# First matmul of the last two token tiles partly in seven block products, a reordered head, and padded value rows, in a fused attention and MLP kernel

## The chip, the cores and the metric

The kernel runs on one core of one Trainium2 chip. Times are device microseconds (us) of that core; with one core it is also the slowest core. Every run quoted here was fast, with a mean granted TensorE clock of 0.988 to 1.0. A "profile" is one execution recorded by the hardware profiler; its span is 1.8 us shorter than the time of the same execution.

Engines are called as the profile calls them: PE is TensorE, DVE VectorE, ACT ScalarE, SP the engine whose queue issues the transfers.

## The reference, cut to what matters

```python
# q, k, v: (8 batches, 8 heads, 576 tokens, 64), float32
q_s = softmax(q, axis=-1); k_s = softmax(k, axis=2)
kv  = einsum('bhsd,bhse->bhde', k_s, v)
x   = einsum('bhsd,bhde->bhse', q_s, kv)          # -> (8, 576, 512)
xn  = (x - mean(x)) / sqrt(var(x) + 1e-6) * g_ln  # over the 512 columns
out = x + relu(xn @ w_ch1) @ w_ch2                # 512 -> 2048 -> 512
```

## The kernel before

Each batch is a tile of 512 tokens. The 64 tokens that each of the eight batches has left over form a ninth tile, "batch 8", done last. The mean is not subtracted from x but from the rows of w1 ("centring", on PE with a matrix of ones and on DVE with a subtraction), and the factor 1/sqrt(var) is applied at the end. Inputs of batch b+1 are loaded and its attention is done inside the matmuls of batch b.

The second matmul already uses the seven-product form (Strassen in Winograd's arrangement): operands cut into 2 x 2 blocks, seven block products in place of eight, and sums of blocks on DVE. The first matmul is plain:

```python
def mm1(c, split, open_=()):
    ...
    for n, m in enumerate(order):                  # 16 output tiles of 128 x 512
        def f(...):
            for ko in range(k0, KO1):              # KO1 = 4
                nc.tensor.matmul(bank[gi], w1_sb[:, ko, m * P : m * P + P], xt[:, ko], ...)
        ids.append(plan.add("PE", 0.216 * (KO1 - k0), f, r=..., w=[(bk, gi)]))
        relu_evac(m, bank[gi], (bk, gi), eng(n))   # PSUM -> hT, mostly on ACT
        if split and n in (HK, KO2 - 1):
            sums(0 if n == HK else 4)              # block sums of hT for the second matmul
```

All work is written as tasks with an engine, a planned time, reads and writes. A list scheduler turns them into one fixed order; each engine then executes its own part of it strictly in that order. A priority (`cls`), a planned delay (`slack`), a planned transfer size (`mb`) or an `after=` changes only that order, and it can change it far from where it was written.

```python
class Plan:
    def add(self, eng, dur, fn, r=(), w=(), cls=1, land=0.0, mb=0.0, after=(), slack=0.0): ...
    def emit(self):
        seq = self.order()                         # the list scheduler
        for i in seq: ... self.tasks[i][2]()       # issue

def load(dst, src, w, mb):                         # one queue, on SP, in order
    gate[1] = plan.add("SP", 0.55, lambda: nc.sync.dma_start(dst, src), w=w, mb=mb, land=0.65,
                       after=tuple(gate[0]) + ((gate[1],) if gate[1] is not None else ()))
```

The part of the input side that the argument needs, for a batch in the steady state. `gate[0]` holds the loads of a batch behind the transposing transfer of the batch before it:

```python
if steady:
    gate[0] = state["eqT"]                         # the eqT transpose of the batch before
lq = [load_half(b, q, hf) for hf in range(2)]      # SP: load q
for hf in range(2):
    queries(hf, lq[hf])                            # ACT: exp; DVE: sum, reciprocal, eq = eq * rzq
...
state["eqT"] = (dma_t(),)                          # SP: eqT <- eq, a transposing transfer
# later: PE k-v product, ACT/DVE kve scaling, PE eqT x kve, ACT copies to xsT,
# SP: x <- xsT, a transposing transfer; DVE: bn_stats of x
```

The parts of the head that the change reorders are `load_w1` (a w1 tile scaled on ACT or DVE) and `centre_w1`:

```python
def load_w1(blk):
    on_act = ((1,), (0, 1, 3), (1,), (1, 3))[blk]  # which of four tiles ACT scales
    ...
def centre_w1(blk):
    def f():
        for ko in range(KO1):
            nc.tensor.matmul(bank, ones, w1_sb[:, ko, cs], start=(ko == 0), stop=(ko == KO1 - 1))
    plan.add("PE", 0.216 * KO1, f, ...)
    state["nm"] = plan.add("ACT", ..., lambda: nc.scalar.copy(nm, bank), ...)
    ...                                            # DVE: w1 = w1 - nm
```

The softmax here doesn't subtract the row's maximum and nothing guards it: scores larger than these inputs give would overflow.

Of the kernel before, what the change touches and what calls it, by code (L numbers as in the profile page):

```python
# [13 lines left out]
FP16 = mybir.dt.float16  # L14
BF16 = mybir.dt.bfloat16
U32 = mybir.dt.uint32
AF = mybir.ActivationFunctionType
# [122 lines left out]
def kernel(  # L140
# [29 lines left out]
    def sb(shape, dt, name):  # L170
        return persist.tile(shape, dt, name=name, tag=name)
# [10 lines left out]
    ek = [sb([P, 2, JT, P], BF16, f"ek{i}") for i in range(2)]  # L182
    vb = [sb([P, 2, JT, 2, VW], FP16, f"vb{i}") for i in range(2)]
    eq = [sb([P, 2, JT, P], BF16, f"eq{i}") for i in range(2)]
# [70 lines left out]
    def load_w1(blk):  # L255
        on_act = ((1,), (0, 1, 3), (1,), (1, 3))[blk]
        cls = 0.5 if blk else 0
        for kp in range(2):
            s = nxt("stg", NST)
            load(stg[s][:, :1024].rearrange("p (a n) -> p a n", a=2),  # L260
                 w1_src[:, 2 * kp : 2 * kp + 2, blk * 512 : blk * 512 + 512], sk(s), 0.524 if blk or kp else 0.72)
            for a in range(2):
                ko = 2 * kp + a
                after = state["kve"] if blk == 1 and (kp or ko not in on_act) else ()
                if blk == 2:
                    after = (state["nm"],) if ko in on_act else state["ev"][1]
                dst = w1_sb[:, ko, blk * 512 : blk * 512 + 512]
                src = stg[s][:, a * 512 : a * 512 + 512]
                gk = g_sb[:, ko : ko + 1]
                if ko in on_act:  # L270
                    plan.add("ACT", act_t(512, 0.1), lambda dst=dst, src=src, gk=gk: nc.scalar.activation(  # L271
                        dst, src, AF.Copy, scale=gk), r=sk(s) + [("g", ko)], w=[("w1", blk, ko)], after=after, cls=cls)
                else:
                    plan.add("DVE", dve_t(512, 2), lambda dst=dst, src=src, gk=gk: nc.vector.tensor_scalar_mul(
                        dst, in0=src, scalar1=gk), r=sk(s) + [("g", ko)], w=[("w1", blk, ko)], after=after, cls=cls)

    def centre_w1(blk):

        if blk:
            gi = nxt("pa", 4)  # L280
            bank, bk = pa[gi], ("pa", gi)
        else:
            bank, bk = pg[opened[2]], ("pg", opened[2])
        cs = slice(blk * 512, blk * 512 + 512)
        wk = [("w1", blk, ko) for ko in range(KO1)]
        def f():
            for ko in range(KO1):
                nc.tensor.matmul(bank, ones, w1_sb[:, ko, cs], start=(ko == 0), stop=(ko == KO1 - 1))  # L288
        plan.add("PE", 0.216 * KO1, f, r=wk + ["ones"], w=[bk], cls=0)
        state["nm"] = plan.add("ACT", act_t(512), lambda: nc.scalar.copy(nm, bank), r=[bk], w=["nm"], cls=-0.5)  # L290
        def sub(k0, k1, m0, m1):
            n = (m1 - m0) * P
            c0 = blk * 512 + m0 * P
            return plan.add("DVE", dve_t((k1 - k0) * n, 2), lambda: nc.vector.tensor_tensor(  # L294
                w1_sb[:, k0:k1, c0 : c0 + n], w1_sb[:, k0:k1, c0 : c0 + n],
                nm[:, m0 * P : m0 * P + n].unsqueeze(1).to_broadcast([P, k1 - k0, n]), op=ALU.subtract),
                r=["nm"] + wk, w=[("w1c", 4 * blk + m, k) for m in range(m0, m1) for k in range(k0 // 2, k1 // 2)], cls=0)

        if blk == 0:
            state["sub"] = sub(0, 2, 0, 4)  # L300
            return lambda: sub(2, 4, 0, 4)
        sub(0, 4, 0, 1)
        sub(0, 4, 1, 4)

# [18 lines left out]
    def attn(b, kind, between=None, exps=(), sums_=(), kvs=()):  # L323
# [44 lines left out]

        def keys(hf, s):
            plan.add("ACT", act_t(QW), lambda: nc.scalar.activation(  # L370
                ek[u][:, hf].rearrange("p j (s d) -> p s j d", s=2), sv(s), AF.Exp),
                r=sk(s), w=[("ek", u, hf)], cls=cls, slack=late, after=exps)
# [10 lines left out]
        def kv(hs):  # L383
            ab = [[nxt("pa", 4) for _ in range(2)] for _ in hs]
            def f():
                for n, hf in enumerate(hs):
                    for j in range(JT):
                        for e in range(2):
                            for i in range(2):
                                r0, c0 = R * e, D * i  # L390
                                nc.tensor.matmul(pa[ab[n][e]][c0 : c0 + D, :VW], ek[u][r0 : r0 + R, hf, j, c0 : c0 + D],  # L391
                                                 vb[u][r0 : r0 + R, hf, j, i, :], start=(j == 0), stop=(j == JT - 1))
            ids = []
            kcls = 0 if not steady else 0.35 if b > 2 else -0.6
            plan.add("PE", 0.1 + 0.42 * len(hs), f, r=[("ek", u, h) for h in hs] + [("vb", u, h, i) for h in hs for i in range(2)],
                     w=[("pa", a) for x in ab for a in x], cls=0, slack=SLACK if steady else 0.2, after=kvs)
            for n, h in enumerate(hs):
# [58 lines left out]
        if kind == "first":  # L456
            lq, lk, lv = [load_half(b, t, 0, x) for t, x in ((q, 0), (k, 0), (v, 0))]
            queries(0, lq)
            keys(0, lk)
            values(0, lv)  # L460
            lq = load_half(b, q, 1)
            load_w1(0)
            pe_t_evac(0, *pe_t(0))
            kves = kv([0])
            xT([0])
            queries(1, lq, kves[:1])
            t1 = pe_t(1)
            between()
            pe_t_evac(1, *t1, (state["sub"],))
            lk, lv = [load_half(b, t, 1) for t in (k, v)]  # L470
            keys(1, lk)
            values(1, lv)
            cnt["pa"] = 0
            state["kve"] = kv([1])
            state["sub2"]()
            xT([1])
            return xT_last
# [58 lines left out]
    def relu_evac(m, bank, bk, eng):  # L536
# [4 lines left out]
        if eng == "ACT":  # L541
            plan.add("ACT", act_t(512), fa, r=[bk], w=[("hT", m)], cls=0)
        else:
            plan.add("DVE", dve_t(512), fd, r=[bk], w=[("hT", m)], cls=0)

# [35 lines left out]

    def sums(k0):
        n = 4
# [3 lines left out]
        h12, h22 = hT[:, kh, 0:256], hT[:, kh, 256:512]  # L587
        lo, hi = [("hT", k0 + i) for i in range(n)], [("hT", HK + k0 + i) for i in range(n)]
        sk = lambda i: [("S", i, k0 + j) for j in range(n)]
        def tt(i, a, b, op, r):  # L590
            plan.add("DVE", dve_t(256 * n, 2), lambda: nc.vector.tensor_tensor(S[i][:, ks], a, b, op=op), r=r, w=sk(i), cls=0.3 if k0 else 0.45)  # L591
        tt(0, h21, h22, ALU.add, lo + hi)
# [34 lines left out]
    def mm2_split(c):  # L627
# [3 lines left out]
        if c == B:  # L631
            ga[1] = (pa[0][:, 0:256], ("pa", 0))
        o1, o2 = nxt("ot", NOT), nxt("ot", NOT)
        rk = lambda t0: [(stk, "r", 2 * t0), (stk, "r", 2 * t0 + 1)]
        hk = lambda k0: [("hT", k0 + k) for k in range(HK)]
        skey = lambda i: [("S", i, k) for k in range(HK)]
        wk = lambda k0: [("w2", k0 + k) for k in range(HK)]
        tkey = lambda i: [("T", i, k) for k in range(HK)]
        h = lambda k, t0, i: hT[:, k, 256 * t0 + i * P : 256 * t0 + i * P + P]
        A = {"11": (lambda k, i: h(k, 0, i), hk(0)), "12": (lambda k, i: h(HK + k, 0, i), hk(HK)),  # L640
             "22": (lambda k, i: h(HK + k, 1, i), hk(HK))}
        for i in range(4):
# [5 lines left out]

        def product(a, b, g, first, last):
            (fa, ka), (fb, kb) = A[a], Bm[b]  # L650
            for i, ks in [(0, range(0, 4)), (0, range(4, HK)), (1, range(HK))]:
                def f(i=i, ks=ks):
                    for k in ks:
                        nc.tensor.matmul(g[i][0], fa(k, i), fb(k),  # L654
                                         start=(first and k == 0 and (i == 0 or g[0][1] != g[1][1])), stop=(last and k == HK - 1),
                                         skip_group_check=True)
                plan.add("PE", 0.1093 * len(ks), f, r=[ka[k] for k in ks] + [kb[k] for k in ks], w=[g[i][1]])

# [27 lines left out]
        add_x(2, gb, 1, 256)  # L686
        product("S3", "T3", ga, False, False)
        state["stats"] = (final(o2, 1, ga, 2, 1),)
        if c == B:
            plan.add("SP", 0.62, lambda: nc.sync.dma_start(last_rows(1)[:, :, 256:512], ot[o2][:, :, 256:512]),  # L690
                     r=[("ot", o2, 1)], mb=0.26, land=2.0, cls=0)
        product("S4", "22", gb, False, True)
        final(o1, 1, gb, 1, 0)
# [14 lines left out]
    def mm2(c):  # L708
# [4 lines left out]
        for k0 in range(0, KO2, 4):  # L713
            for j in range(J):
                def f(k0=k0, j=j):
                    for kk in range(k0, k0 + 4):
                        nc.tensor.matmul(pg[gis[j]], hT[:, kk, j * P : j * P + P], w2_sb[:, kk, :],  # L717
                                         start=(kk == 0), stop=(kk == KO2 - 1))
                i = plan.add("PE", 0.864, f, r=[("hT", kk) for kk in range(k0, k0 + 4)] + [("w2", kk) for kk in range(k0, k0 + 4)], w=[("pg", gis[j])])
                if j == 0:  # L720
# [22 lines left out]
    def warm(n):  # L743
        return plan.add("PE", 0.43 * n, lambda: zeros(pg[3], True)(n), r=["zero"], w=[("pg", 3)], cls=0)


# [28 lines left out]
    for b in range(B):  # L775
        if b:
            state["tok"] = tokens(b, 0.7 if b > 1 else 0.35, stats=state["stats"])
        if b == B - 1:
            tokens(8, 0.7, stats=state["stats"])
        rstd = state.get("rstd")  # L780
        ids = mm1(b, b > 0, () if b else opened)
        if b == 0:
# [11 lines left out]
        before = (ids[-1], rstd)  # L794
    mm1(8, True)
    mm2_split(8)
# [36 lines left out]
```

## Time and profile before

| | before |
|---|---|
| time, median of 3 runs | 279.06 us (278.26 to 279.40) |
| the profiled execution | 277.7 us, span 275.9 |
| PE, DVE, ACT busy | 97%, 72%, 61% of the span |
| start of batch 1 on PE | 52.25 us |
| k-v product of batch 7 starts on PE | 201.52 us |
| end of PE's work | 272.08 us |

The stretches of the profiled execution, by one view of all engines (start and end in us, length, then for PE, PEld, DVE, ACT, POOL the busy us and the instructions, the granted clock, the busy share of the DMA engines, GB/s):

```profile
46.00:72.00 26.00, 26.00 (x268) 14.45 (x266) 23.76 (x47) 19.20 (x35) 0.00 (x0) 1.00 0.93 255
72.00:118.00 46.00, 46.00 (x456) 29.09 (x446) 36.14 (x76) 33.72 (x55) 0.00 (x0) 1.00 0.83 220
118.00:202.00 84.00, 83.96 (x828) 54.03 (x818) 62.70 (x133) 56.43 (x91) 0.00 (x0) 1.00 0.78 205
```

Read the first busy number against the length: from 46 to 202 us PE has work for all but 0.04 us.

### The profile page before, as it was taken

Reading aid. Unit: us, or ns where it says so; the run is one execution under the profiler, and the core shown is the slowest. Engines: PE = TensorE matmul, PEld = TensorE weight load, DVE = VectorE, ACT = ScalarE, POOL = GpSimd, SP = SyncE. Lnnn points to the kernel's source line nnn. Section 1 sums busy time; section 2 is a strip of 40 time slices with the busy share of each in tenths; the row PEclk is TensorE's granted clock in tenths of the full one; section 3 lists DMA queues with packets and bytes.
Section 4 is the critical chain, followed back from the end, with each engine's and each line's share of the span. In section 5 each row is a group of like instructions: output and inputs, shape, how many; then the busy total and the mean of one; then the engine's idle time right before and its main releaser. Section 6 shows DMA issues by size and latency. Waiting matters only on the chain.

```text
span 275.9 us, 5670 instructions
## 1 busy us (share of the span) xinstructions
PE 268.4 (97%) x2324; PEld 163.7 (59%) x2324; DVE 198.5 (72%) x412; ACT 168.2 (61%) x274; POOL 1.7 (1%) x12
## 2 busy tenths in 40 slices
PE   8988999999999999999999999999999999999994
PEld 3433445446864587458745874578457845874583
DVE  1788998998769767966697669766976764742562
ACT  4678966788598693659466856685664076016500
POOL 2000000000000000000000000000000000000000
PEclk9999999999999999999999999999999999999999
DMA  7999999799989994499659965796544450022004
GB/s 257 361 386 387 388 388 233 184 330 256 319 265 187 280 334 48 143 216 389 75 153 185 395 100 154 160 394 124 154 86 77 78 154 0 0 64 90 1 4 152
DMA packets 55874, 54.83 MB, mean 199 GB/s; under 512 B 34596, under 2 KB 35112, under 8 KB 55848
## 3 DMA queue, kind: packets, MB, share of 16 engines
q1 hardware_dynamic: 55696, 54.34, 69.6%
q8 instruction: 18, 0.29, 0.4%
q10 hardware_dynamic: 152, 0.13, 0.1%
q14 instruction: 8, 0.07, 0.1%
HBM read 36.70 MB, written 9.44 MB: 167 GB/s over the span
## 4 chain that ended last, share of the span: by engine, by line
PE 91%; DMA 4%; SPq 1%; ACT 1%; DVE 1%; issue 0%
PE pg L575 43%; PE pg L654 35%; PE pg L717 5%; DMA stg<-in_v_dram 4%; PE pa L391 2%; PE pa L422 2%; PE pa L654 1%; PE pa L575 1%; SPq L238 1%; PE pa L288 1%; PE pg L553 1%; ACT hT L538 1%; PE pa L445 0%; PE pa L519 0%; DVE vb L377 0%; ACT w_sb L271 0%
## 5 line engine op out<-in xcount | busy, mean ns | idle before, releaser
L538 ACT ACTIVATE hT<-pg 128x512 f16<-128x512 f32 x134 | 78.8, 598 | 65.2 <-PE pg L575 64.8
L575 PE MATMUL pg<-xsT,w_sb 128*128 128x512 f16 x488 | 108.4, 379 | 0.8 <-ACT hT L538 0.8
L575 PEld LDWEIGHTS <-w_sb 128*128 128x128 f16 x568 | 54.8, 98 | 65.9 <-DVE w_sb L294 1.6
L654 PEld LDWEIGHTS <-S 128*128 128x128 f16 x512 | 49.6, 98 | 6.3 <-issue 0.4
L654 PE MATMUL pg<-T,S 128*128 128x256 f16 x368 | 41.9, 273 | 0.0
L654 PEld LDWEIGHTS <-hT 128*128 128x128 f16 x384 | 37.2, 98 | 7.8 <-issue 2.2
L591 DVE TENSOR_TENSOR S<-hT 128x1024 f16<-128x1024 f16 x32 | 21.8, 681 | 26.5 <-ACT hT L538 26.5
L664 DVE SCALAR_TENSOR_TENSOR cp<-pg,st,x 128x256 f32<-128x256 f32 x46 | 20.2, 479 | 14.2 <-PE pg L654 13.7
L664 DVE SCALAR_TENSOR_TENSOR ot<-pg,st,cp 128x256 f32<-128x256 f32 x47 | 20.5, 477 | 12.2 <-PE pg L654 12.0
L654 PE MATMUL pg<-w_sb,hT 128*128 128x256 f16 x248 | 29.2, 273 | 0.0
L527 DVE BATCH_NORM_STATS2 bst<-x 128x6 f32<-128x512 f16 x36 | 23.9, 666 | 4.8 <-DMA x<-xsT 4.8
L342 DVE TENSOR_REDUCE zq<-eq 128x18 f32<-128x1152 bf16 x16 | 21.5, 1344 | 4.7 <-ACT eq L340 4.7
L340 ACT ACTIVATE eq<-stg 128x1152 bf16<-128x1152 f32 x16 | 18.7, 1170 | 7.3 <-DMA stg<-in_q_dram 7.2
L346 DVE TENSOR_TENSOR eq<-eq,rzq 128x1152 bf16<-128x1152 bf16 x16 | 21.6, 1352 | 0.3
L370 ACT ACTIVATE ek<-stg 128x1152 bf16<-128x1152 f32 x16 | 18.7, 1170 | 3.0 <-DMA stg<-in_k_dram 3.0
L380 ACT CAST vb<-stg 128x1152 f16<-128x1152 f32 x15 | 17.6, 1174 | 4.4 <-DMA stg<-in_v_dram 4.3
L435 ACT CAST xsT<-pa 128x512 f16<-128x512 f32 x31 | 16.0, 592 | 3.0 <-PE pa L422 3.0
L654 PE MATMUL pg<-w_sb,S 128*128 128x256 f16 x128 | 15.3, 273 | 0.0
L717 PE MATMUL pg<-w_sb,hT 128*128 128x512 f16 x64 | 14.8, 380 | 0.0
L654 PE MATMUL pg<-T,hT 128*128 128x256 f16 x120 | 14.4, 273 | 0.0
L575 PE MATMUL pg<-xT,w_sb 128*128 128x512 f16 x64 | 14.0, 379 | 0.0
L740 PE MATMUL pg<-zero 128*128 128x512 f16 x33 | 10.6, 481 | 1.2 <-DVE zero L223 1.2
(71 smaller groups left out, 162.6 us busy)
## 6 DMA issues: line engine op xcount, KB each, us to landing
stg<-in_q_dram SPq DMA_DIRECT2D x16, 576.0 KB, 5.3
stg<-in_k_dram SPq DMA_DIRECT2D x16, 576.0 KB, 7.2
stg<-in_v_dram SPq DMA_DIRECT2D x16, 576.0 KB, 9.0
out_dram<-ot SPq DMA_DIRECT2D x33, 256.0 KB, 3.7
stg<-in_moe_w_ch_dram SPq DMA_DIRECT2D x16, 512.0 KB, 10.8
out_dram<-ot SPq DMA_DIRECT2D x1, 512.0 KB, 2.8
out_dram<-ot SPq DMA_DIRECT2D x1, 128.0 KB, 2.7
out_dram<-ot ACTq DMA_DIRECT2D x1, 128.0 KB, 2.2
```

The costliest lines, as they stand in the source:

```text
L340: plan.add("ACT", act_t(QW), lambda: nc.scalar.activation(e.rearrange("p j (s d) -> p s j d", s=2), sv(s), AF.Exp), r=sk(s), w=[("eq", u, ...
L342: plan.add("DVE", dve_t(QW), lambda: nc.vector.reduce_sum(zq[:, hf], eh, axis=AX.X), r=[("eq", u, hf)], w=[("zq", hf)], cls=qcls, after=sums_)
L346: plan.add("DVE", dve_t(QW), lambda: nc.vector.tensor_tensor(eh, eh, rzq[:, hf].to_broadcast([P, 2 * JT, D]), op=ALU.mult), r=[("rzq", hf) ...
L370: plan.add("ACT", act_t(QW), lambda: nc.scalar.activation(ek[u][:, hf].rearrange("p j (s d) -> p s j d", s=2), sv(s), AF.Exp), r=sk(s), w= ...
L380: plan.add("ACT", act_t(QW), lambda: nc.scalar.copy(vd, va), r=sk(s), w=[("vb", u, hf, i) for i in range(2)], cls=cls, slack=late, after=t ...
L527: plan.add("DVE", dve_t(512), lambda j=j: nc.vector.bn_stats(bst[:, j, :], x[:, j, :]), r=[(xk, j)], w=[("bst", j)], cls=cls, slack=2.0 if ...
L538: nc.scalar.activation(hT[:, m, :], bank, AF.Relu)
L575: nc.tensor.matmul(bank[gi], w1_sb[:, ko, m * P : m * P + P], xt[:, ko], start=(ko == 0), stop=(ko == KO1 - 1))
L591: plan.add("DVE", dve_t(256 * n, 2), lambda: nc.vector.tensor_tensor(S[i][:, ks], a, b, op=op), r=r, w=sk(i), cls=0.3 if k0 else 0.45)
L654: nc.tensor.matmul(g[i][0], fa(k, i), fb(k), start=(first and k == 0 and (i == 0 or g[0][1] != g[1][1])), stop=(last and k == HK - 1), ski ...
L664: nc.vector.scalar_tensor_tensor(dst[:, i, :], in0=g[i][0], scalar=sti[:, 4, 2 * t0 + i : 2 * t0 + i + 1], in1=src[:, i, :], op0=ALU.mult, ...
L717: nc.tensor.matmul(pg[gis[j]], hT[:, kk, j * P : j * P + P], w2_sb[:, kk, :], start=(kk == 0), stop=(kk == KO2 - 1))
```

## The change

It has three parts.

1. *Tail.* In batches 7 and 8, two of four groups of output tiles of the first matmul are computed as seven block products. Sums of w1 blocks (once) and of x blocks (per batch) are made on DVE, the intermediate sums leave PSUM through ACT copies and DVE additions. The readiness of hT, the first matmul's output, is now tracked by halves of its tokens, and one product and the statistics of batch 8 get another place in the order. The aim is less PE work.
2. *Head.* ACT takes more of the w1 scaling, several `after=` and planned times change, centring of the first block is cut in halves. The aim is that PE saturates earlier.
3. *Padding.* The rows of the value tile grow from 65 to 66 elements.

```diff
-    vb = [sb([P, 2, JT, 2, VW], FP16, f"vb{i}") for i in range(2)]
+    vb = [sb([P, 2, JT, 2, VW + 1], FP16, f"vb{i}") for i in range(2)]
...
-        on_act = ((1,), (0, 1, 3), (1,), (1, 3))[blk]
+        on_act = ((0, 1), (0, 1), (1,), (1, 3))[blk]
...
-                after = state["kve"] if blk == 1 and (kp or ko not in on_act) else ()
+                after = state["kve"] if blk == 1 and ko else ()
                 if blk == 2:
-                    after = (state["nm"],) if ko in on_act else state["ev"][1]
+                    after = (state["nm"],) if ko in on_act else (state["subs"],) if kp else state["ev"][1]
...
-        plan.add("PE", 0.216 * KO1, f, r=wk + ["ones"], w=[bk], cls=0)
+        for k0, k1 in ((0, 2), (2, 4)) if blk == 0 else ((0, 4),):
+            ...
+            plan.add("PE", 0.216 * (k1 - k0), f, r=wk[k0:k1] + ["ones"], w=[bk], cls=0)
...
-            queries(1, lq, kves[:1])
+            queries(1, lq, kves)
...
-            keys(1, lk)
+            keys(1, lk, (state["nm"],))
...
+    UNITS[7] = UNITS[8] = (0, 1)
+    def w1_sums(n, before): ...        # four sums of w1 blocks of group n, DVE, 128 x 512 each
+    def x_sums(c): ...                 # four differences of x blocks, DVE, 128 x 512 each
+    def mm1_seven(c):
+        ...
+            for u in us:
+                u.product("11", "11", 0, True, False)   # 4 matmuls of 256 columns into bank 0
+                u.copy(0, 0)                            # ACT: PSUM -> SBUF
+                u.product("12", "21", 1, True, True)
+                u.end(1, 0, 0, 0)                       # DVE: bank + copy -> hT, then the maximum with 0
+            for u in us:
+                u.product("S2", "T2", 0, False, False)
+                u.copy(0, 1)
+                u.product("S1", "T1", 2, True, False)
+                u.copy(2, 2)
+            for u in us:
+                u.product("S3", "T3", 0, False, False)
+                u.end(0, HK, 1, 2)
+                u.product("S4", "22", 2, False, True)
+                u.end(2, 0, 1, 1)
+            for u in us:
+                u.product("22", "T4", 0, False, True)
+                u.end(0, HK, 0)
...
-    mm1(8, True)
+    mm1_seven(8)
```

## The prediction

> **What bounds the kernel now.** I read the page first (shares, slices, chain of waits), then the chain in order of time, then the timelines of TensorE, VectorE (DVE) and ScalarE (ACT) in the head (0 to 36 us) and from 205 us to the end. The page says that TensorE (PE) is busy for 97% of the span and carries 91% of the chain:
>
> ```profile
> PE 268.4 (97%) x2324; PEld 163.7 (59%) x2324; DVE 198.5 (72%) x412; ACT 168.2 (61%) x274; POOL 1.7 (1%) x12
> PE 91%; DMA 4%; SPq 1%; ACT 1%; DVE 1%; issue 0%
> ```
>
> PE's busy time counts matmuls on a zero tile in the head, so I looked for where real work becomes continuous. PE's timeline (start us, us, what, count, idle before it):
>
> ```profile
> 13.89 1.03 PE L288 MATMUL pg<-w_sb,ones 128*128 128x512 f16 x4
> 15.86 0.68 PE L360 MATMUL pa<-ident_b,eq 128*128 128x128 bf16 x9 [0.94 <-DVE eq L346]
> 20.57 1.90 PE L575 MATMUL pg<-xsT,w_sb 128*128 128x512 f16 x8
> 23.23 1.90 PE L575 MATMUL pg<-xsT,w_sb 128*128 128x512 f16 x8 [0.76 <-ACT hT L538]
> 24.96 1.03 PE L288 MATMUL pa<-w_sb,ones 128*128 128x512 f16 x4
> 26.69 1.03 PE L288 MATMUL pa<-w_sb,ones 128*128 128x512 f16 x4
> ```
>
> The last gap ends at 23.23; from there to 272.09 the chain is PE almost without a break. So the time is (when PE saturates) + (PE work after it) + a short tail. In the tail the first matmul of the last two batches (L575) and the second (L654) alternate in the chain (start, length, what):
>
> ```profile
> 219.95 13.81 PE pg L575 x64
> 233.76 12.23 PE pg L654 x112
> 245.99 13.81 PE pg L575 x64
> ```
>
> Two prices follow: 13.81 / 64 = 0.2158 us per matmul with 512 columns, and 12.23 / 112 = 0.1092 us per one with 256. The second matmul is already in the seven-product form at this price. Halving the width costs 2 x 0.1092 - 0.2158 = 0.003 us per pair, almost nothing.
>
> In the head, PE waits for what DVE does in the wrong order. DVE's timeline:
>
> ```profile
> 11.51 0.48 DVE L274 TENSOR_SCALAR w_sb<-stg,g_sb 128x512 f16<-128x512 f32 x1 [0.61 <-DMA stg<-in_moe_w_ch_dram]
> 11.91 0.28 DVE L409 TENSOR_SCALAR kve<-pa,rz 128x64 f16<-128x64 f32 x1
> 15.83 0.75 DVE L377 CAST vb<-stg 128x576 f16<-128x576 f32 x1
> 22.35 0.49 DVE L274 TENSOR_SCALAR w_sb<-stg,g_sb 128x512 f16<-128x512 f32 x1 [0.87 <-DMA stg<-in_moe_w_ch_dram]
> 22.75 1.28 DVE L294 TENSOR_TENSOR w_sb<-w_sb,cp 128x512 f16<-128x512 f16 x2
> ```
>
> The subtraction at 22.75 is what PE's matmul at 23.23 needs, and it stood behind a weight scaling that waited 0.87 us for a transfer it has nothing to do with. (The waits view names ACT for that gap; ACT's relu of the bank ended earlier, so I take it for DVE.)
>
> **What the skill says.** "TensorE: Matmul & The Clock Gate", Back-to-back issue gap: warm, N/2.4 + 2.5 ns, so 109.2 ns at 256 and 215.8 at 512. The trace agrees to the digit (0.1092, 0.2158), not with the 131 ns which that section gives for sustained streams at 512. "VectorE: DVE Perf Modes", tier table: tensor_tensor on 16-bit SBUF data runs at 2x, with a PSUM operand at 1x. The trace agrees: the 128x1024 f16 sums at L591 take 0.69 us, the 128x512 operation out of PSUM at L731 0.68 (2.72 for four). "Advanced Engine Details and Errata", 2x-2p Requirements: source and destination need an outermost dimension even in both, or odd and equal in both. The v cast in the head reads one run of 576 and writes 9 rows of 64, so it doesn't qualify; at 0.75 us = 0.15 + 576/960 it indeed runs at 1x, while the L310 casts (1024 in one run on both sides) run at 2x, 0.69. Padding the row from 65 to 66 leaves 9 rows of 64.
>
> **The change, part by part.**
>
> *PE in the last two batches.* Of four groups of four output tiles, two use seven products of 4 matmuls of 256 columns: 7 x 4 x 0.1092 = 3.058 us, in place of 16 x 0.2158 = 3.453. Saved 0.395 a group, four groups in all: 1.58 us. This lies on the path, if nothing stalls PE.
>
> *ACT in one such batch.* Before: 16 relus of 0.60 in 13.81 us. After: 6 copies PSUM to SBUF, 4 relus out of place or in place on the DVE sums, 2 relus from PSUM, 8 direct relus: 20 x about 0.57 = 11.4 us, plus 0.5 of statistics in batch 7, against 13.03 us of PE. Full, but it fits.
>
> *DVE in one such batch.* Added: 6 sums out of PSUM x 0.68 = 4.1, two in-place maxima of about 0.3, four x differences of 0.42 (the L605 price): 6.4 us. Before, DVE was busy 15.4 us of 26.0 in batch 7 and less in batch 8, so it fits. The eight w1 sums (8 x 0.42 = 3.4 us) stand in the instruction order in batch 5's second half, where DVE idles 0.43, 1.16, 0.87 and 0.87 us between evacuations, and the first x differences in the same gaps of batch 6.
>
> *Does PE stall there?* I followed PE's queue from the start of batch 7 (= 0). PE writes a first product to bank A, ends at 0.44, does two more products, and adds to bank A again at 1.31. ACT's copy of A must lie between: start 0.48 (the trace shows PE's end to ACT's start as 0.04), end 1.08. Margin 0.2 us, the smallest. Later copies end at 1.62, 2.39, 2.93, 3.70, 4.24 and are needed at 2.62, 3.50, 3.93, 4.37, 4.81. DVE first ends batch 7's statistics (the fourth ends at 221.65 before, which is 1.70 on this clock, so 1.7 to 2.0), then its sums end at about 2.7, 3.3, 4.65, 5.3, 5.9, 6.6; PE needs the last four at 5.25, 5.68, 6.55, 7.85. The relus of the two banks used again come at 6.5 and 7.6, needed at 9.6 and 8.7. Batch 8 gives the same picture without the statistics. So no stall, or a few tenths: 0 to 0.4.
>
> *The head.* Instruction counts and transfers stay; the order changes. ACT takes a second w1 scaling, so DVE's second kve no longer waits behind the transfer at 11.51. Two of four opening groups go before the second k-v product. DVE no longer scales the late w1 tile before the subtraction. Walking it with the durations above: first centring copy (ACT) 14.35 to 14.95 (15.41 to 15.98 before), eq product done at 15.4, opening matmuls from about 16.1, second x product at 18.5 (19.07), second centring from 19.5 (19.41), the eight continuing matmuls from 20.4 (20.57), then the subtraction at 21.5 to 22.75 (22.75 to 24.0), so the next group at 22.1 (23.23). The fourth centring then starts at 25.85 against 26.69, with the same work done before it: PE is 0.85 us ahead. The new order confirms this in another way: behind the head, one group of 4 matmuls (0.86 us) now stands before each k-v product of batch 1, as it would if PE arrives earlier and the inputs do not.
>
> *Given back.* At the end of batch 0 only 0.86 + 0.19 us of PE work now stand between the last x product and batch 1, where ACT needs two copies of 0.54: 0.1 to 0.3 us may be lost.
>
> *Padding.* No effect: the cast stays at 0.75, the k-v matmuls at 0.41 us for 36.
>
> Sum: -1.58 + 0.2 - 0.85 + 0.2 = -2.0 us, so 279.06 - 2.0 = 277.0.
>
> **Rivals.** (1) The head's lead is lost, because transfers bind it: DMA is 94% busy up to 23.2 us and 100% from there to 52 us, and batch 1's v lands as late as 44.95 us. For: ACT waits on DMA many times in this stretch. Against: PE shows no wait on those inputs, and the new order puts other work in front. It would leave the tail's gain only: 277.5. (2) ACT or DVE becomes the bound in the two last batches; a copy or a sum late by half a microsecond is paid two to four times, and the gain turns to 0 or +1: 278 to 279. For: ACT is 11.9 of 13.0 us full, and queues are in order, so one wait of ACT for DVE's statistics holds everything behind it. Against: the walk has margins of 0.2 to 2 us. (3) The DVE extras in batches 5 and 6 delay an evacuation and hold a PSUM bank: +0.3 to 1. Against: they fit the gaps shown. (4) Padding speeds the v cast or the k-v reads: 0.3 us in the head, or with 16 half products up to 1 us over all: 276. No row speaks for it.
>
> **Range and chances.** The timed runs before span 278.26 to 279.40, so +-0.5 is noise of the measure. With the head at 0 to -1.3 and the tail at -1.6 to 0, I put the time at 277.0, from 275.8 to 278.3. Two per cent is 5.6 us, over twice the whole sum of gains, and a loss of that size would need stalls of over 7 us. Faster 0.02, within 2% 0.96, slower 0.02.
>
> **What would show it.** In the profile after: the two stretches of L575 and seven-product work in the tail at 13.0 to 13.2 us each, not 13.81, with no PE wait on ACT or DVE over 0.2; the fourth centring at about 25.85; the step to batch 1 with a PE wait of at most 0.3 on ACT; the v cast at 0.75. Wrong: PE gaps in the tail that sum to over 0.5, a saturation of PE no earlier than before, a cast near 0.45, or k-v products clearly under 0.41.

## The result, and the profile after

The changed kernel took 276.18 us, the median of four runs (275.61 to 276.50), against 278.96 (278.26 to 279.40) for the kernel before. The ratio is 0.990, 95% interval 0.9872 to 0.9929. A ratio here is the mean time of one kernel's fast runs over that of the other's fast runs of the same rounds, so it is not quite the ratio of the medians. By the 2% rule this is "same", as expected, at 0.8 us below the predicted time.

The page's shares and its chain of waits, changed kernel:

```profile
PE 265.8 (97%) x2367; PEld 167.5 (61%) x2367; DVE 211.8 (77%) x444; ACT 170.9 (62%) x282; POOL 1.7 (1%) x12
PE 67%; DMA 21%; DVE 5%; SPq 4%; ACT 1%; issue 1%
```

PE's share of the chain fell from 91% to 67%, and transfers now carry 21%. That is a first sign that PE's own work no longer sets the time alone.

**The tail.** One row per kernel of the view by stretches, from the first PE work of batch 7 to the end of PE. Before:

```profile
219.95:272.09 52.14, 52.12 (x353) 34.26 (x350) 27.56 (x57) 19.65 (x36) 0.00 (x0) 1.00 0.16 47
```

After:

```profile
220.38:270.91 50.53, 50.49 (x400) 38.88 (x398) 37.00 (x77) 22.62 (x44) 0.00 (x0) 1.00 0.17 48
```

The stretch is 1.61 us shorter, with PE busy throughout in both. DVE's work in it grew by 9.4 us and ACT's by 3.0, and neither made PE wait. But look at the two starting times: batch 7 begins 0.43 us *later* after the change.

**The head.** PE's timeline of the changed kernel (start, us, what, count, idle before it):

```profile
21.72 1.04 PE L576 MATMUL pg<-xsT,w_sb 128*128 128x512 f16 x4 [0.54 <-DVE w_sb L295]
22.87 1.90 PE L576 MATMUL pg<-xsT,w_sb 128*128 128x512 f16 x8
24.61 1.89 PE L289 MATMUL pa<-w_sb,ones 128*128 128x512 f16 x8
27.63 2.55 PE L576 MATMUL pg<-xsT,w_sb 128*128 128x512 f16 x11 [0.27 <-DVE w_sb L295]
```

The group that stood at 23.23 us before starts at 21.72. The third and fourth centring are one row of eight at 24.61, so the fourth starts at 24.61 + 4 x 0.216 = 25.47 (26.69 before). There is a new wait of 0.27 us at 27.63, on DVE's subtraction, which the prediction did not have. Batch 1 starts on PE at 51.46 us against 52.25. So the head did gain 0.8 us there, and it is gone before batch 7.

**Where it went.** PE's waits between 50 us and the end, changed kernel (releaser, us in total, times, longest); the same view of the kernel before has no line:

```profile
PE pg L576 <- DVE ot L667: 0.9, 3, 0.4
```

One of the three is at 110.24 us. PE's line there, DVE's timeline ahead of it, and the issue of the transfer that DVE waits for (from SP's timeline), changed kernel:

```profile
97.25 5.55 SPq L525 DMA_TRANSPOSE x<-xsT  x1
106.48 0.69 DVE L528 BATCH_NORM_STATS2 bst<-x 128x6 f32<-128x512 f16 x1 [1.71 <-DMA x<-xsT]
109.33 0.86 DVE L667 SCALAR_TENSOR_TENSOR ot<-pg,st,x 128x256 f32<-128x256 f32 x2
110.24 7.07 PE L576 MATMUL pg<-xsT,w_sb 128*128 128x512 f16 x32 [0.29 <-DVE ot L667]
```

The same places of SP and DVE in the kernel before:

```profile
98.09 4.75 SPq L524 DMA_TRANSPOSE x<-xsT  x1
106.49 0.69 DVE L527 BATCH_NORM_STATS2 bst<-x 128x6 f32<-128x512 f16 x1 [0.88 <-DMA x<-xsT]
109.33 0.86 DVE L664 SCALAR_TENSOR_TENSOR ot<-pg,st,x 128x256 f32<-128x256 f32 x2
```

DVE arrives 0.83 us earlier after the change, and waits 0.83 us longer for the transposing transfer of x. That transfer is issued 0.84 us earlier too, but DVE can start on it at the same time, 9.2 us after the issue in place of 8.4. The statistics stand ahead of the evacuation in DVE's order, so the evacuation at 109.33 starts at the same time too. PE needs its bank and loses the lead.

**Padding.** The v cast of the head, changed kernel:

```profile
15.26 0.75 DVE L378 CAST vb<-stg 128x576 f16<-128x576 f32 x1
```

It is 0.75 us as before, and the 36 k-v products of the head take 0.41 us in both.

### The profile page after: what moved, and what is told of

Same layout as the page of the kernel before. It is cut to its first block, busy times and chain, and to the rows that moved or that the text cites. A ratio compares the mean times of both kernels' runs of the same rounds, so it can differ in the third digit from the quotient of the medians.

```text
span 274.7 us, 5785 instructions
## 1 busy us (share of the span) xinstructions
PE 265.8 (97%) x2367; PEld 167.5 (61%) x2367; DVE 211.8 (77%) x444; ACT 170.9 (62%) x282; POOL 1.7 (1%) x12
## 4 chain that ended last, share of the span: by engine, by line
PE 67%; DMA 21%; DVE 5%; SPq 4%; ACT 1%; issue 1%
PE pg L576 25%; PE pg L656 21%; DMA x<-xsT 9%; DMA stg<-in_moe_w_ch_dram 7%; PE pg L720 5%; DMA stg<-in_v_dram 5%; PE pg L819 3%; SPq L238 3%; PE pa L854 3%; PE pg L854 3%; DVE bst L528 2%; DVE ot L667 2%; PE pa L392 2%; PE pa L576 1%; PE pa L656 1%; PE pa L819 1%
## 5 line engine op out<-in xcount | busy, mean ns | idle before, releaser
L576 PE MATMUL pg<-xsT,w_sb 128*128 128x512 f16 x424 | 95.0, 379 | 1.7 <-DVE ot L667 0.9
L539 ACT ACTIVATE hT<-pg 128x512 f16<-128x512 f32 x110 | 65.0, 597 | 35.1 <-PE pg L576 34.5
L576 PEld LDWEIGHTS <-w_sb 128*128 128x128 f16 x440 | 42.1, 98 | 52.7 <-issue 2.5
L825 ACT COPY stg<-pg 128x512 f32<-128x512 f32 x10 | 5.5, 589 | 14.3 <-PE pg L819 14.2
L592 DVE TENSOR_TENSOR S<-S,hT 128x1024 f16<-128x1024 f16 x16 | 11.1, 691 | 0.5
```

The source lines that it names most:

```text
L539: nc.scalar.activation(hT[:, m, :], bank, AF.Relu)
L592: plan.add("DVE", dve_t(256 * n, 2), lambda: nc.vector.tensor_tensor(S[i][:, ks], a, b, op=op), r=r, w=sk(i), cls=(-0.25 if i < 2 else -0. ...
```

## The experiments

The theory after the first result: **the tail is worth 1.6 us, always, and the head's lead is returned in batches 2 to 5, where what arrives by transfer does not come earlier because PE is earlier.** Rivals: (a) the head is worth its 0.8 us in most executions and the profile was unlucky; (b) DVE's instruction order, not the transfers, eats the lead and moving the statistics would recover it; (c) the padding matters somewhere; (d) the tail is worth more than PE's count says.

Milestones on PE of all profiles (us): the start of batch 1, the start of the k-v products of batches 2, 4 and 7, and the end of PE. Kernels with the new head do eight matmuls of 256 columns more before the product of batch 2 (0.87 us), so that column is not to be compared across heads; the others are. "Idle" is PE's time without work in 46 to 202 us.

| profile | head | batch 1 | kv 2 | kv 4 | kv 7 | end | idle |
|---|---|---|---|---|---|---|---|
| before | old | 52.25 | 71.40 | 117.62 | 201.52 | 272.08 | 0.04 |
| changed | new | 51.46 | 71.49 | 117.24 | 201.95 | 270.88 | 0.91 |
| changed, again (1) | new | 51.73 | 71.76 | 119.27 | 202.84 | 271.77 | 1.48 |
| tail only (2) | old | 52.47 | 71.61 | 117.78 | 202.61 | 271.54 | 0.77 |
| head only (3) | new | 51.81 | 71.84 | 118.37 | 202.94 | 273.50 | 1.29 |
| statistics behind (4) | new | 51.91 | 71.94 | 117.64 | 204.07 | 273.00 | 2.09 |
| delayed (5) | new | 52.79 | 72.82 | 118.85 | 203.03 | 271.96 | 0.75 |
| unpadded (6) | new | 51.93 | 71.96 | 118.08 | 201.76 | 270.69 | 0.27 |
| changed, q first (7) | new | 51.58 | 71.61 | 121.60 | 205.18 | 274.11 | 2.97 |
| before, q first (8) | old | 52.26 | 71.40 | 120.32 | 203.90 | 274.46 | 2.69 |
| changed, q first late (9) | new | 51.76 | 71.79 | 118.78 | 202.36 | 271.29 | 0.96 |
| before, q first late (10) | old | 52.17 | 71.31 | 117.48 | 201.06 | 271.62 | 0.00 |
| changed, third time (11) | new | 51.97 | 72.00 | 117.53 | 203.16 | 272.10 | 1.25 |
| tail only, q first late (12) | old | 52.06 | 71.21 | 117.46 | 201.04 | 269.97 | 0.00 |

Runs 1 to 4 shared one chip and its runs of the kernel before (median 278.19 us), 5 to 8 another (278.09), 9 to 12 a third (279.09). All outputs were correct. Each kernel was timed in five rounds.

### 1. The changed kernel again

No edit.

> The changed kernel unaltered, as the yardstick for the three runs beside it. Two theories of where the 2.8 us between the medians come from. Theory A (transfers pace the middle): the last two batches give 1.6 us; the head puts TensorE 0.8 us ahead, and the middle takes that away again, because the transposed x of batches 3 to 5 lands no earlier and the VectorE statistics that wait for it stand ahead of the evacuations that TensorE needs. Theory B (the lead stays): 1.6 from the tail plus 0.8 to 1.2 from the head, and the waits in the profiled run were an unlucky execution. Both: about 276.2 us, ratio 0.990.

Measured: 276.66 us (276.19 to 277.38), ratio 0.9942 [0.9922, 0.9963], which is 1.5 us between medians where the first pair had 2.8. The profile lost its lead in another place than the first. PE's timeline, and ACT's ahead of it:

```profile
77.78 0.62 PE L423 MATMUL pa<-eqT,kve 64*64 64x512 bf16 x7 [1.26 <-ACT kve L406]
```

```profile
74.85 1.16 ACT L341 ACTIVATE eq<-stg 128x1152 bf16<-128x1152 f32 x1 [5.35 <-DMA stg<-in_q_dram]
76.36 1.16 ACT L341 ACTIVATE eq<-stg 128x1152 bf16<-128x1152 f32 x1 [0.34 <-DMA stg<-in_q_dram]
77.43 0.50 ACT L406 ACTIVATE kve<-pa,rz 128x64 f16<-128x64 f32 x2
```

PE waits for the kve scaling. ACT could have done it earlier, but two exponentials of the next q stand ahead of it in ACT's order, and the first waited 5.35 us for its transfer. Three profiles of this one kernel show that exponential starting at 72.03, 74.85 and 72.49 us (the first, this one and run 11). SP issued the loads at 67.36, 67.78 and 67.82, so from issue to the start of the exponential it is 4.7, 7.1 and 4.7 us in executions of the same program.

### 2. The tail's part alone

The head's edits and the padding are taken back, the tail's stay:

```diff
-        on_act = ((0, 1), (0, 1), (1,), (1, 3))[blk]
+        on_act = ((1,), (0, 1, 3), (1,), (1, 3))[blk]
... (and so on for each edit of the head)
```

> The seven products in the last two batches with the head of the kernel before (its order of instructions and its unpadded v rows). Theory A: nearly the whole gain, 276.5 to 277.4, no worse than 0.8 us behind the whole change. Theory B: 277.4 (1.6 us faster than before), about 1.2 us behind the whole change. In the profile the last two batches take 50.5 us from their first matmul to the end of TensorE under both.

Measured: 276.92 us (275.91 to 277.15), ratio 0.9941 [0.9920, 0.9962]. Within the noise, that is the whole of the change's gain in the same rounds (0.9942).

### 3. The head's part alone

```diff
-        ids = mm1_seven(b) if b in UNITS else mm1(b, b > 0, () if b else opened)
+        ids = mm1(b, b > 0, () if b else opened)
...
-    mm1_seven(8)
+    mm1(8, True)
```

> The new head and the padded v rows, with the first matmul of the last two batches as before. Theory A: 278.5 to 279.0, that is 0 to 0.4 us faster than before; in the profile TensorE is 0.8 us ahead at the start of batch 1, shows waits on VectorE's evacuations in batches 3 to 5, and is level with before at the start of batch 7. Theory B: 277.8 to 278.2, 0.8 to 1.2 us faster, with the lead kept to the end.

Measured: 278.14 us (277.49 to 279.36), ratio 0.9996 [0.9971, 1.0021]. The absolute time lies in theory B's range only because the kernel before took 278.19 in these rounds; the difference between the two, 0.05 us, is theory A's. The head brings nothing to the end that these runs can show, although batch 1 starts 0.44 us earlier in its profile. PE's waits from 50 us to the end in that profile:

```profile
PE pg L576 <- DVE ot L667: 1.3, 4, 0.4
```

This is the wait of the first result again, in a kernel without the tail's extra DVE work, so the new sums are not its cause. Nor does it need the lead: run 2, with the old head, shows it too (0.8 us, twice, the first at 139.4 us). PE and the transfers are so near each other there that either head can run into them. Runs 2 and 3 together speak against rivals (a) and (d), within their intervals: run 3's just excludes a head worth 0.8 us (its lower end, 0.9971, is 0.8 us), but a head worth 0.3 us would not be seen.

### 4. The statistics behind the evacuations

The statistics of batches 3 to 5 are moved in the final order behind the last two evacuations; nothing but DVE's order changes.

```diff
+        for ids, last in self.behind:              # in emit, after order()
+            early = [i for i in seq[: seq.index(last)] if i in ids]
+            seq = [i for i in seq if i not in early]
+            at = seq.index(last) + 1
+            seq[at:at] = early
...
+        if c in (3, 4, 5):
+            plan.behind.append((set(range(n0, len(plan.tasks))), state["last"]))
```

> The changed kernel with one thing moved on VectorE: in batches 3, 4 and 5 the statistics of x stand behind the two last evacuations of the batch before, not between and ahead of them. No other engine's order changes. Theory A: TensorE's three waits on those evacuations (0.3 to 0.4 us each in the profile of the changed kernel) go, and 0.7 to 1.2 us are won over the changed kernel: 275.0 to 275.5. Theory B: nothing, within 0.2 us of the changed kernel. A third possibility: the statistics then end later and hold up something else, so that the waits come back in another place and the time is equal.

Measured: 278.54 us (277.24 to 278.99), ratio 1.0001 [0.9978, 1.0023], slower than the changed kernel by 1.9 us between medians, which none of the three expected outcomes had. PE's waits on DVE are gone from the profile, and another took their place:

```profile
PE pa L452 <- ACT xsT L442: 1.9, 5, 0.7
```

ACT's timeline ahead of one of them:

```profile
126.04 1.16 ACT L347 ACTIVATE eq<-stg 128x1152 bf16<-128x1152 f32 x1 [2.51 <-DMA stg<-in_q_dram]
127.11 1.05 ACT L442 CAST xsT<-pa 128x512 f16<-128x512 f32 x2
```

In the changed kernel's first profile this exponential starts at 124.05, after a wait of 0.93 us. With the evacuations in front, DVE's product eq x rzq comes later, so the eqT transpose goes out later on SP's queue, so the q loads gated behind it do too, and ACT's copies stand behind the exponential. This is a loop through four queues, each in order. Rival (b) falls in this form: relieving one queue tightened the next.

### 5. PE delayed on purpose

```diff
+                    if (k0, j) == (0, 0):      # second matmul of batch 0, first group, done twice
+                        for kk in range(4):
+                            nc.tensor.matmul(pg[gis[j]], hT[:, kk, ...], w2_sb[:, kk, :],
+                                             start=(kk == 0), stop=(kk == 3))
```

> The changed kernel with four matmuls of 512 columns done twice at the start of batch 0's second matmul: 4 x 0.2158 = 0.86 us of extra TensorE work on the path of the head, about as much as the head's lead, at the same result. Theory A (the middle is paced by transfers, so a lead or a delay before it is absorbed): 0 to 0.3 us slower than the changed kernel. Theory B (TensorE bounds all the way): 0.86 us slower.

Measured: 277.30 us (276.54 to 278.80), ratio 0.9969 [0.9944, 0.9993]. Against run 6 of the same rounds, the changed kernel but for the padding (276.11, 0.9925), the 0.86 us of added work cost about 1.2 us; the two intervals do not overlap. Theory A's 0 to 0.3 us was wrong. In the milestones it starts batch 1 at 52.79 (0.86 behind run 6) and reaches batch 7's k-v product at 203.03 (1.27 behind). A delay in the head is passed on, and in runs 1 to 3 a lead was not. Both can hold if the arrival is set by the later of PE and the transfers, and the two are near each other. At batch 1's k-v product they are: its second half needs a cast of v that waits for v's load. In run 6 the cast ends at 46.35 and PE starts that half at 46.85; in run 5 it is 46.34 and 47.71.

### 6. Without the padding

```diff
-    vb = [sb([P, 2, JT, 2, VW + 1], FP16, f"vb{i}") for i in range(2)]
+    vb = [sb([P, 2, JT, 2, VW], FP16, f"vb{i}") for i in range(2)]
```

> The changed kernel with the v rows back at 65 elements; every engine's order stays. The prediction said that padding does nothing: equal to the changed kernel within 0.3 us, the v cast of the head at 0.75 us in both, the k-v products at 0.41 us for 36. If padding helped the k-v reads, the k-v stretches would be longer here and the time up to 1 us more.

Measured: 276.11 us (275.66 to 276.74), ratio 0.9925 [0.9908, 0.9942]. The v cast on DVE took 0.754 us, against 0.752 with padding and 0.753 before the change; the v casts on ACT 1175 ns, against 1159 padded. Rival (c) falls in the size that was named: the time is 0.07 us below the lowest of the padded kernel's three medians (276.18, 276.66, 276.71), which come from other rounds, and the ratio is between theirs (0.990 to 0.9942).

### 7 and 8. The q loads ahead of the eqT transpose

This cuts the loop of run 4 at SP's queue: the eqT transpose of a batch goes behind the next batch's two q loads, for the changed kernel (7) and for the kernel before (8).

```diff
         lq = [load_half(b, q, hf) for hf in range(2)]
+        if b > 2:
+            plan.behind.append((set(gate[0]), gate[1]))   # gate[0]: the eqT transpose
```

> The changed kernel with one thing moved on the issuing queue: in batches 2 to 6 the two loads of the next batch's q stand ahead of the transpose of exp(q), which waits for VectorE, not behind it. Theory A in its sharper form (the loop through the queue paces the middle: VectorE's product, transpose, loads behind it, ScalarE's exponentials and VectorE's statistics, evacuations): q, k, v and the transposed x land some 2 to 4 us earlier, TensorE's waits in batches 2 to 5 go, the head's lead stays, and the time is 0.7 to 1.5 us below the changed kernel, about 275.3. If the middle is bound by the bandwidth of the transfers and not by their place in the queue, the loads move but nothing is gained: within 0.2 us. Rival: the transpose itself comes later and TensorE's x product waits for it; slower.

> The same move in the kernel before. The head's work sets TensorE's pace there from 23.2 us on, and in its profile TensorE waited in the middle for 0.04 us only, but its timed runs spread by 1.6 us. Theory A: 0.2 to 0.8 us faster than before (the unlucky executions go), and less of it than in the changed kernel, so that the whole change is worth 2.0 to 2.6 us between the two kernels with q first, against 1.6 without.

Measured: run 7 279.49 us (277.55 to 279.75), ratio 1.0029 [1.0003, 1.0054]; run 8 281.62 us (279.76 to 282.99), ratio 1.0111 [1.0079, 1.0144]. Both were slower. In run 7 the rival of its expectation came true; in run 8 it was not foreseen at all. PE's only wait after 50 us in run 7:

```profile
97.26 0.63 PE L429 MATMUL pa<-eqT,kve 64*64 64x512 bf16 x8 [2.97 <-DMA eqT<-eq]
```

In batch 3 eqT is what PE needs first, and now it comes later. The matmuls that follow this wait, run 7 and then run 8:

```profile
97.82 5.33 PE L664 MATMUL pg<-w_sb,hT 128*128 128x256 f16 x32
98.20 3.67 PE L662 MATMUL pg<-w_sb,hT 128*128 128x256 f16 x32
```

They are the same 32 matmuls. In run 7 they took 1.66 us longer, and the clock granted from 97.26 to 103 us was 0.69 to 0.71; in run 8's profile it was 1.00. So run 7's profile lost to the clock as well as to the wait. Five of its six runs, this one among them, had a mean clock of 0.994 (279.10 to 279.75 us), the sixth 1.0 (277.55). That the others had the same dip, and why it came, is not shown. But after this wait PE does not wait again: from the k-v product of batch 4 to that of batch 7 it takes 205.18 - 121.60 = 83.58 us = 3 x 27.86. That is PE's own work for three batches. The changed kernel's first profile took 84.71 for it. Run 8 shows the same two numbers (a wait of 2.69 us at 97.64, then 83.58). Part of run 8's timed loss goes with a lower clock too: four of its runs had a mean granted clock of 0.988 to 0.993 (281.54 to 282.99 us), and two, the profiled one among them, 0.998 (279.76 and 280.06). The medians of the two runs differ by 2.1 us, inside the 2.0 to 2.6 that were expected, but with such clocks this confirms nothing.

### 9 to 12. The same, from batch 5 on only

The reordering leaves batch 3 and 4 alone and is put into the changed kernel (9), the kernel before (10) and the tail alone (12), beside the changed kernel once more (11).

```diff
-        if b > 2:
+        if b > 4:
             plan.behind.append((set(gate[0]), gate[1]))
```

> The changed kernel with the two query loads put ahead of the eqT transpose on the sync engine's queue, but only from the queries of batch 5 on, where the transfers are no longer at 99% of their time and the batch that paid 3 us in the earlier run of this order is left as it was. Theory (the head's lead is lost to loads that stand in line behind the eqT transpose, and to evacuations that stand behind the resulting late work): the waits of the matmul engine in batches 4 to 6 go, so that the k-v product of batch 7 follows that of batch 4 by 83.6 us (three times 27.86; 84.7 in the changed kernel's first profile, 83.6 to 84.6 in its relatives) and the time is 0.3 to 1.1 us under the changed kernel of the same rounds: about 275.5, ratio to the kernel before 0.988 to 0.992. Rival (the rest of the lead is lost to transfers whatever the order): the same time as the changed kernel within 0.3 us, with the waits elsewhere.

> The kernel before with the same reordering. Its matmul engine loses only 0.3 us between the k-v products of batch 4 and 7 (83.90 against 83.58). Theory: at most 0.3 us faster, ratio 0.999 to 1.001, so the reordering is worth something only where there is a lead to keep. If it gains as much as the changed kernel does, the reordering is a gain of its own and says nothing about where the lead went.

> The changed kernel once more, as the comparison for these rounds. Expected 276.2 to 276.7, ratio to the kernel before 0.990 to 0.995.

> The tail's part of the change alone (head of the kernel before) with the same reordering. Theory: its period of 83.6 us from the k-v product of batch 4 to that of batch 7 as well (it was 84.8 in the earlier profile of the tail alone), and the end 0.3 to 0.8 us behind the changed kernel with the reordering, which is the head's lead, kept at last. Rival (the head's lead is lost before batch 4 whatever comes later): the same time as the changed kernel with the reordering, within 0.2 us.

| run | us, median and range | ratio to before | kv 4 to kv 7 |
|---|---|---|---|
| 9: changed, q first late | 276.61 (275.57 to 277.37) | 0.9906 [0.9874, 0.9937] | 83.58 |
| 10: before, q first late | 277.46 (277.23 to 278.04) | 0.9943 [0.9915, 0.9972] | 83.58 |
| 11: changed | 276.71 (276.07 to 277.71) | 0.9915 [0.9882, 0.9947] | 85.63 |
| 12: tail only, q first late | 276.23 (275.61 to 277.63) | 0.9902 [0.9869, 0.9935] | 83.58 |

The part of the expectation about the trace held in all three kernels: no wait from batch 4 to batch 7, 83.58 us each. The part about the time held in none of the two main runs. The changed kernel gained 0.1 us between medians where 0.3 to 1.1 was expected, and the kernel before gained 1.6 where at most 0.3 was expected. Run 12 was 0.4 us faster than run 9, where 0.3 to 0.8 us slower was expected.

Why run 9 did not gain, in its profile: it lost its lead ahead of batch 4. Stretches of run 9:

```profile
46.00:72.00 26.00, 26.00 (x228) 14.55 (x230) 23.96 (x48) 19.13 (x35) 0.00 (x0) 1.00 0.88 255
72.00:118.00 46.00, 45.04 (x449) 28.35 (x434) 35.42 (x75) 32.79 (x53) 0.00 (x0) 1.00 0.85 243
118.00:202.00 84.00, 84.00 (x795) 54.14 (x794) 66.42 (x141) 55.63 (x91) 0.00 (x0) 1.00 0.76 192
```

PE is without work for 0.96 us in 72 to 118 us and full after that. The first of its waits is run 1's:

```profile
77.27 0.62 PE L429 MATMUL pa<-eqT,kve 64*64 64x512 bf16 x7 [0.72 <-ACT kve L412]
```

ACT's exponential in front of that kve started at 74.35 us, after waiting 4.83 us for q. In the kernels with the old head that exponential starts at 72.03 to 72.36 us (the profiles of before and runs 2, 10 and 12). In those with the new head, and with SP's order in that stretch unchanged, it starts at 72.03 to 74.85 (the changed kernel, runs 1, 3 to 6, 9 and 11). So although PE comes earlier with the new head, this transfer comes no earlier, and on average 0.9 us later (73.1 against 72.2, run 5 with its delay left out). About 0.2 us of that is a later issue of the loads, the rest a slower landing, above all in runs 1 and 9. ACT's order differs there as well: the old head has one kve scaling between the two exponentials, the new one has both behind them.

Why the loads are issued no earlier can be read from the traces. SP has them behind the eqT transpose, and that is issued 19.3 to 19.4 us after batch 1's first k-v product in all 14 profiles. PE starts this product at 44.73 to 45.07 us in the five profiles of the old head and at 45.01 to 45.52 in the eight of the new head without the delay. The reason is in the new order: one more group of four matmuls of batch 0 (0.86 us) stands ahead of the product. Lines of the kernel before and of the changed one:

```profile
35.33 9.66 PE L717 MATMUL pg<-w_sb,hT 128*128 128x512 f16 x44
44.91 0.48 PE L391 MATMUL pa<-vb,ek 64*64 64x65 f16 x36
34.55 10.52 PE L720 MATMUL pg<-w_sb,hT 128*128 128x512 f16 x48
45.01 0.48 PE L392 MATMUL pa<-vb,ek 64*64 64x65 f16 x36
```

So up to here the lead is work that PE took forward, and what hangs on batch 1's attention does not come earlier. An order with the product first was not run. The second cast of v ends at 45.89 in the changed kernel and PE uses it at 46.39, so an estimate from these two numbers is that 0.5 us at most could be had there before v's load binds.

Run 12, with the old head, shows what a loop without waits is worth. Its stretches:

```profile
72.00:118.00 46.00, 46.00 (x457) 29.10 (x454) 36.45 (x76) 33.85 (x55) 0.00 (x0) 1.00 0.88 244
118.00:202.00 84.00, 84.00 (x824) 54.23 (x810) 66.53 (x142) 55.46 (x91) 0.00 (x0) 1.00 0.79 193
```

Its profiled execution took 275.61 us. Run 10's took 277.23, also without a wait. The difference is 1.62, the tail's gain once more. The medians of the two differ by 1.2.

Run 10 also says something about the measure. The kernel before loses about 1.6 us in an ordinary timed run of these rounds to what the reordering removes, and its profile (0.04 us of idle PE) does not show that: the profiled execution, of an earlier set of rounds, was 1.4 us faster than the median of these rounds. No profile of a slower execution of the kernel before was taken, so which wait it has there is not shown.

No kernel here beats the changed one beyond doubt. Runs 9, 11 and 12 lie within 0.5 us of each other, with intervals that overlap.

## Why the prediction was right or wrong

The predicted 277.0 us, its range and "within 2%" hold: 276.18, and 276.66 and 276.71 when repeated. Term by term:

- **Tail, -1.58 us: right.** Measured -1.61 on the stretch itself. From batch 7's k-v product to the end it is 70.56 us in the kernel before, in run 3 and in run 10, which have the old tail. It is 68.93 in the changed kernel and in runs 1, 2, 5, 6, 9, 12 (and 68.94 in 11). So the term is 1.63, in every execution, whatever the head did. The work counts (16 x 0.2158 against 28 x 0.1092 a group) account for all but 0.05 us.
- **Stalls in the tail, +0.2: too careful.** PE had no wait there. The walk through the queues gave margins of 0.2 us and more, and they were kept; the ACT copies took 0.58 to 0.62 us and the DVE additions 0.68 to 0.69 on average, near the 0.60 and 0.68 that were assumed. (The line from which the prediction took 0.68, L731, is a SCALAR_TENSOR_TENSOR; the additions are the TENSOR_TENSOR with a PSUM operand that it meant.)
- **Head, -0.85 us, less 0.2 given back at batch 1: right in size up to batch 1, partly by luck, and wrong at the end.** The lead at batch 1 was 0.79 us in the first profile, and 0.3 to 0.8 in all profiles of this head without the added delay (averages: 51.8 against 52.2 us). The way there was not the predicted one: the fourth centring came 1.22 us earlier and not 0.85 (25.47 against 26.69), the unforeseen wait at 27.63 took some 0.4 of it back, and the loss of 0.2 on ACT's copies at batch 1 did not come. The step that failed is the one that carried it from there to the end unchanged, on the ground that PE showed no wait on later inputs. The prediction also took the extra group ahead of batch 1's k-v products as a confirmation of the lead; it is the reason why the work that hangs on these products is not ahead (45.01 against 44.91). Three comparisons within the same rounds give the head's part 0.04% at most, in either direction (run 1 against 2, run 3 against before, run 9 against 12), with intervals of some 0.25%, or 0.7 us, to each side. So a small remainder of the lead is not excluded; the predicted one shows nowhere, and at batch 7's k-v product no profile of the new head is earlier than that of the kernel before. What took its place in the profiles is the prediction's own first rival, that transfers bind, together with the order in which the other engines wait for them. The prediction turned that rival down because the profile of before shows no PE wait on a transfer. But a PE that is just in time shows none either. The signs of it were DVE's 0.88 us and ACT's 2.3 us of waiting for transfers at the points where they stand ahead of something PE needs, and they were already there to read. Not tested is a rival to this: the new head also changes the order of ACT, DVE and PE up to batch 2, and that order by itself may cost what the lead gains.
- **Padding, 0: right.** The cast stayed at 0.75 us. The reason given, the odd count of rows, fits but was not tested by a layout with an even count.
- **The sum, -2.0 us.** The parts that the runs establish give -1.6. The measured differences of medians were -2.8, -1.5 and -2.4 us. No run ties the rest to a part of the change: the median of the kernel before moved between 278.1 and 279.1 from one set of rounds to the next, while that of the changed kernel stayed within 0.5 us. That the changed kernel avoids some of what slows the kernel before in such rounds is possible and not shown. So the first result, 0.8 us better than predicted, is no evidence of a hidden gain of the head, and that the sum came so near is in part luck: it has 0.65 us from a head that gave none that can be seen. The prediction took +-0.5 us of spread for the time before, which was about right for one set of runs and too little for the base that the sum was put on.

What stays open is how the waits are shared out in ordinary, unprofiled executions. It is shown where they lie in single profiles, and that they sit at three places: the kve scaling in batch 2, the xsT copies from batch 2 on (runs 1, 5, 6 and 9 wait for them at 80 to 82 us, run 11 at 184), the evacuations from batch 3 on. How much of the head's lead would remain if all three were cured was not reached: the fastest of all runs with the new head and the new tail was 275.57 us, and the kernel with the old head reached 275.61.

## What to carry to other kernels

The work removed at the end of this kernel, where PE waited for no transfer, was worth its price to a few hundredths of a microsecond; a lead won at the start has to survive every place where something arrives on its own schedule. Before counting such a lead, look in the engines that feed the critical one for waits on transfers that stand ahead of something it needs: a lead can just lengthen such a wait (0.88 us became 1.71 here), and moving the waiting instruction can tighten the next queue instead. Compare the profiled execution's own time with the timed runs before taking a wait, or the lack of one, as typical.

## What the Trainium skill lacked or had wrong

- "TensorE: Matmul & The Clock Gate", Back-to-back issue gap, gives about 131 ns per matmul of 512 columns for sustained streams and calls N/2.4 + 2.5 ns the isolated figure. Here long sustained streams run at the latter: 13.81 us for 64 matmuls, 215.8 ns each, and 109.2 ns at 256 columns.
- "DMA: Bandwidth & Descriptors", Where 436 GB/s comes from, says that the HBM side, about 358 GB/s, binds transfers between HBM and SBUF. The slices of the head, where weights and inputs are loaded, show 385 to 389 GB/s here, with one core at work. The figure is a stack's rate divided between two cores, so it is the condition that this passage lacks; two cores at once were not run.
- None of the pages tells what an in-order engine costs when an instruction that waits for a transfer stands ahead of others: 5.35 us of waiting in ACT became 1.26 us in PE (run 1), and 0.83 us of lead in DVE became none (the first result).
- None tells how far the landing of one transfer can vary between executions of the same program while the queues are full: 4.7 to 7.1 us from the issue of the same q loads to their first use, in three executions of the changed kernel.
